# Mask by matmul up to pair 19, by copied gate sums from pair 20 on, and the later order planned again

## The chip, the cores and the metric

The kernel runs on one core of a Trainium2 chip. The metric is the device time of one execution in microseconds (us). The kernel before was timed in three runs: 425.29, 425.94 and 428.68, with the median 425.94. One further execution was taken by the profiler, and the traces below are from that one.

## The reference

Two layers follow each other. The first is attention with forgetting gates: 8 batches, 8 heads, 576 positions, head dimension 64. The second is a SwiGLU feed-forward block on 4608 tokens, 512 wide inside and 1536 wide in the middle.

```python
scores = scale * q @ k.T
cum = cumsum(log(clip(f, 1e-4, 1)))
decay = cum[:, :, :, None] - cum[:, :, None, :]
scores = where(causal, -1e9, scores + decay)     # causal: key after query
attn = exp(scores - max(scores)); attn = attn / (sum(attn) + 1e-9)
x = (attn @ v)  # heads side by side: 4608 x 512
out = (silu(x @ w_gate) * (x @ w_val)) @ w_out
```

The gate sum of the query's own position is the same for a whole row of scores, so the softmax drops it. Only the sum at the key has to be added.

## The kernel before, in words

Attention goes by 32 pairs of heads, two heads of one batch each. A pair has nine blocks of 64 queries; the two heads lie on the 128 partitions, so that one score matmul of a block `i` gives 128 rows by 64(i+1) keys. A pair is worked on in two groups: g = 0 holds the blocks 0 to 3, g = 1 the blocks 4 to 8. The scores are written with the opposite sign, so that a row's minimum is looked for and the exponential takes scale -1.

The steps of one pair are these.

- SyncE loads k, q and the pair's gate sums (`cb`, one row for each head, repeated on 64 partitions). GpSimd casts k and q to bf16 (`kb`, `qb`, L433 and L431), TensorE transposes them (L447), and ScalarE or VectorE copies the result out (`kt`, `qz`, L459 and L461).
- `scores` (L480): TensorE multiplies into one of two score banks (`sp`, L493). VectorE adds the gate sums, writes the sum into `t` and reads out the minimum of each row (L517, one custom instruction and one read of its accumulator). ScalarE takes the exponential and its row sum (L532).
- `normalize` (L538): VectorE makes the reciprocal of the sums (L548, L550), GpSimd scales the exponentials to bf16 (`pk`, L568), and the result is transposed: on TensorE for pairs 0 to 7 (L598), by one DMA transpose a pair for the others (L581).
- `weighted` (L606): TensorE multiplies with v (L624), and ScalarE or VectorE copies the result to the ring `xT` (L648).

The causal mask concerns only the last 64 keys of each block, the diagonal. There are two ways for it, and `MFROM` is the pair from which the second is used:

- Below `MFROM`, TensorE adds the mask to the scores: after each block's last score matmul comes one more, with the identity as weights and the mask of 64 columns as the moving side (L497). VectorE can then take the whole block in one instruction.
- From `MFROM` on, `copies` (L468) makes `cm`, the pair's gate sums plus the mask, once for all nine blocks, on VectorE or GpSimd (L476). VectorE then takes the diagonal 64 keys of a block by an instruction of its own that reads `cm` and goes on from the minimum of the part before it. Of the nine blocks, seven (1 to 7) are cut in two by this; block 0 is all diagonal, and block 8 has its diagonal in another bank in any case.

The feed-forward layer runs between: `gate` (L691) multiplies with the two weights (L706), ScalarE takes a tanh (L712), VectorE makes two products (L714, L717); `project` (L720) multiplies with the third (L734), and the result leaves through ScalarE or VectorE (L741, L743) and SyncE (L746).

The order of all this is fixed before the launch by `Plan.order` (L62). It takes a planned duration for each operation on each engine that may run it, a latency behind it, the buffers, and a priority; it plays the work through, always taking the operation that can start first, and writes the instructions of each engine in that order. Each engine keeps its order on the chip and waits where an operand isn't there. `NUDGE` (L259) shifts the priority of named units: a9.0 is pair 9, group 0; q is a pair's loading and transposing; f and o are tiles of the feed-forward layer. So a planned duration that is altered changes where everything behind it stands.

Of the kernel before, what the change touches and what calls it, by code (L numbers as in the profile page):

```python
# [8 lines left out]
F32 = mybir.dt.float32  # L9
BF16 = mybir.dt.bfloat16  # L10
AF = mybir.ActivationFunctionType
ALU = mybir.AluOpType
# [2 lines left out]
BIG = 1.0e9  # L15
HUGE = 3.0e38
COLD = 25000


class Op:  # L20
# [11 lines left out]
class Plan:  # L32
# [29 lines left out]
    def order(self):  # L62
# [72 lines left out]
        while ready:  # L135
            best = None
            for n, r in ready.items():
                o = self.ops[n]
                got = room(o, r)
                if got is None:  # L140
                    continue
                for e, dur in o.engs.items():
                    s = max(r, got[0], free[e])
                    for k in o.reads:
                        if k in using and using[k][0] != e:
                            s = max(s, using[k][1])
                    c = (s + o.bias.get(e, 0), o.prio, n, e, dur, got[1])
                    if best is None or c[:4] < best[:4]:
                        best = c
            if best is None:  # L150
                raise RuntimeError("no operation can start: " + ", ".join(str(self.ops[n].writes) for n in list(ready)[:20]))
            s, _, n, e, dur, take = best
            o = self.ops[n]
            s -= o.bias.get(e, 0)
            if e == "PE" and s < COLD:
                dur *= 2
            for k, b in take:
                name = self.home[k]
                self.where[k] = b
                slots[name][b] = k  # L160
                taken[name, self.line[k]] += 1
            o.start, o.eng = s, e
            free[e] = s + dur
            for k in o.reads:
                if self.home.get(k) in self.banks:
                    using[k] = e, s + dur + 30
            if o.dma:
                q = e == "POOL"
                at = max(wire[q], s + (2550 if q else 2000))
                both = max(0, min(2 * o.dma, wire[not q] - at))  # L170
                wire[q] = at + o.dma + both / 2
                wire[not q] += both / 2
                if o.ring:
                    free[e] = max(free[e], wire[q] - 1450)
                o.end = wire[q] + 1100
            else:
                o.end = free[e] + o.lat
            for k in {*o.writes, *o.reads, *o.holds}:
                left[k] -= 1
                until[k] = max(until[k], o.end)  # L180
            del ready[n]
            for kid in kids.get(n, ()):
                waiting[kid.n] -= 1
                if not waiting[kid.n]:
                    ready[kid.n] = max(d.end for d in kid.deps)
            done.append(o)
# [10 lines left out]
def kernel(  # L197
# [12 lines left out]
    B, H, S, D = q.shape  # L210
# [3 lines left out]
    P = 128  # L214
# [19 lines left out]
             [[(8, 0, 512)], [(8, 512, 576), (6, 0, 448)], [(7, 0, 512)], [(5, 0, 384)], [(4, 0, 320)]]]  # L234


    MFROM = 12
    CMENG = ("POOL", "DVE")

    ON_PE = {(p, g) for p in range(8) for g in range(2)}  # L240

    NDIRECT = 0
    NSEL = 1
    MOST = (("p", 1), ("o", 2), ("f", 3))
# [11 lines left out]
    HEAD = "10 00 20 30 11 01 31 21"  # L256


    NUDGE = "a21.0:1 a31.1:10 f5:1 f7:4.5 o8:2 q11:-2 q15:4 q24:2.5"  # L259

    WAIT = ""
    ORDER = [(int(u[0]), int(u[1])) for u in HEAD.split()]
# [32 lines left out]
    for i in range(0, NB, 2):  # L295
        bufs(f"e{i}", [P, QB * (i + 2)], F32, 2)
    bufs("eo", [P, 512], F32, 4)
    bufs("tm", [P, NB + 1], F32, 6)
    bufs("ls", [P, NB, 2], F32, 6)
    bufs("lr", [P, NB], F32, 6)  # L300
    both = {}
    for n in ("pk", "pT"):
        both[n] = [sb.tile([P, sum(NSL), P], BF16, name=f"{n}{x}") for x in range(2)]
# [114 lines left out]
    def prepare(p):  # L418
        s = first[p]
        for name in ("k", "q"):  # L420
# [4 lines left out]
            def cast(e, name=name, fk=fk, bk=bk, KR=KR):  # L425
# [5 lines left out]
                    eng[e].tensor_scalar(dst, src, -scale, 1.0, op0=ALU.mult, op1=ALU.mult)  # L431
                else:
                    eng[e].tensor_copy(dst, src)  # L433
            engs = {"POOL": 850}
            if p < NPB:
                engs = {"POOL": 850, "ACT": 850, "DVE": 500} if name == "k" else {"POOL": 1050, "ACT": 1050, "DVE": 680}
            o = pl.op(engs, cast, [fk], [bk], s - 1 + (name == "q") * .1)
# [30 lines left out]
    def copies(p):  # L468

        if p < MFROM:  # L470
            return
        pl.key(("cm", p), "cm")

        def add(e):
            src = pl.buf(("cb", p)).rearrange("r (i c) -> r i c", c=QB)
            eng[e].tensor_tensor(pl.buf(("cm", p)), src, maskf.unsqueeze(1).to_broadcast((P, NB, QB)), op=ALU.add)  # L476
        cost = {"POOL": S * 1.05 + 245, "DVE": S / .96 + 82}
        pl.op({e: cost[e] for e in CMENG}, add, [(("cb", p), 3)], [("cm", p)], first[p] - .5, holds=[("cb", p)])

    def scores(p, g):  # L480
        s = at[p, g]
        pl.key(("tm", p, g), "tm")
        pl.key(("ls", p, g), "ls")
        for n, bank in enumerate(BANKS[g]):
            sk = ("sp", p, g, n)
            pl.key(sk, "sp")
            pr = s + n * .05

            def mult(e, bank=bank, sk=sk):
                sp, kt, qz, o = pl.buf(sk), pl.buf(("kt", p)), pl.buf(("qz", p)), 0  # L490
                for i, a, z in bank:
                    last = z == QB * (i + 1)
                    nc.tensor.matmul(sp[:, o:o + z - a], qz[:, i, :, :].rearrange("p h r -> p (h r)"), kt[:, a:z],  # L493
                                     start=True, stop=not last or p >= MFROM)
                    o += z - a
                    if last and p < MFROM:
                        nc.tensor.matmul(sp[:, o - QB:o], ident, mask, start=False, stop=True)  # L497
            cols = [z - a for _, a, z in bank] + [64 for i, a, z in bank if z == QB * (i + 1) and p < MFROM]
            pl.op({"PE": mm(*cols)}, mult, [("kt", p), ("qz", p), (("kt", p), "done"), (("qz", p), "done"), "mask"], [sk], pr, lat=220)
            o = 0  # L500
            cuts = []
            for i, a, z in bank:
                last = z == QB * (i + 1)
                if last and a < QB * i and p >= MFROM:
                    cuts += [(i, a, QB * i), (i, QB * i, z)]
                else:
                    cuts.append((i, a, z))
            for i, a, z in cuts:
                last = z == QB * (i + 1)
                own = last and p >= MFROM  # L510
                tk = ("t", p, i)
                if a == 0:
                    pl.key(tk, "t")

                def add(e, i=i, a=a, z=z, o=o, sk=sk, tk=tk, last=last, own=own):
                    tm = pl.buf(("tm", p, g))
                    nc.vector.tensor_tensor_reduce(  # L517
                        out=pl.buf(tk)[:, a:z], in0=pl.buf(sk)[:, o:o + z - a],
                        in1=pl.buf(("cm", p))[:, i, :] if own else pl.buf(("cb", p))[:, a:z], scale=1.0,
                        scalar=HUGE if a == 0 else tm[:, NB:NB + 1], op0=ALU.add, op1=ALU.min,  # L520
                        accum_out=tm[:, i:i + 1] if last else tm[:, NB:NB + 1])
                w = [tk, ("tm", p, g)] + ([("m", p, i)] if last else [("m", p, i, "part")])
                r = [sk] + ([("cm", p)] if own else [(("cb", p), 3)]) + ([("m", p, i, "part")] if a else [])
                pl.op({"DVE": (z - a) / .96 + (142 if a else 82)}, add, r, w, pr, lat=100, holds=[] if own else [("cb", p)])
                o += z - a
                if last:
                    ek = ("e", p, i)
                    pl.key(ek, epool(i))

                    def exp(e, i=i, tk=tk, ek=ek):  # L530
                        L = QB * (i + 1)
                        nc.scalar.activation(pl.buf(ek)[:, :L], pl.buf(tk)[:, :L], AF.Exp,  # L532
                                             bias=pl.buf(("tm", p, g))[:, i:i + 1], scale=-1.0,
                                             accum_out=pl.buf(("ls", p, g))[:, i, 0:1])
                    sums[p, g] = pl.op({"ACT": QB * (i + 1) * .833 + 290}, exp, [tk, ("m", p, i)], [ek, ("ls", p, g)],
                          pr, lat=150, holds=[("tm", p, g)])

    def normalize(p, g):  # L538
# [10 lines left out]
        pl.op({"DVE": 95, "ACT": 200}, guard, [("ls", p, g)] + ([("z", "ls", n) for n in range(6)] if p < 3 else []), [("lr", p, g)], s, lat=120)  # L549
        pl.op({"DVE": 95}, lambda e: nc.vector.reciprocal(lr(), lr()), [("lr", p, g)], [("l2", p, g)], s, lat=170, holds=[("lr", p, g)])  # L550
        kk = ("pk", p, g)
        joint = not any((p, x) in ON_PE for x in range(2))
        pl.key(kk, f"pk{g}", same=("pk", p, 1 - g) if joint else None)
        w = HI[g] - LO[g] + 1
        for i in range(HI[g], LO[g] - 1, -1):
# [75 lines left out]
    def spread(p, g, pv):  # L631
# [5 lines left out]
        for a, z in ((0, cut), (cut, w)):  # L637
# [3 lines left out]
            def evac(e, a=a, z=z):  # L641
# [5 lines left out]
                src = bass.AP(src.tensor, src.offset + QB * (z - a - 1), [full[0], [-QB, z - a], full[2]])  # L647
                (nc.scalar.copy if e == "ACT" else nc.vector.tensor_copy)(dst, src)  # L648
            tok = t0 + a * QB, t0 + z * QB
            o = pl.op({"ACT": QB * (z - a) * .833 + 130, "DVE": QB * (z - a) / .96 + 85}, evac, [xk],  # L650
                      [("x", hp, n) for n in range(tok[0] // QB, tok[1] // QB)], s)
            o.bias = LATER if p >= 8 else {}
            evacs.append((pv, tok))
# [1 line left out]
    def load_v(b):  # L655
        for c in range(5):
# [9 lines left out]
                (), [fk], s, dma=1460 if n == P else 800, after=wait)  # L666
            def cast(e, c=c, n=n, fk=fk):
                (nc.scalar.copy if e == "ACT" else eng[e].tensor_copy)(pl.buf(("vt", b))[0:n, c, :, :], pl.buf(fk)[0:n, :, :])
            o = pl.op({"POOL": 670} if b else {"POOL": 670, "ACT": 580, "DVE": 600}, cast,
                  [fk] + ([("z", "vt", b)] if c == 4 and b < 2 else []), [("vt", b), ("vt", b, c)], s + .5)  # L670
            o.bias = SPARE

# [183 lines left out]
```

## Time and profile before

| | |
|---|---|
| median of three runs | 425.94 us |
| profiled execution, own time | 422.99 us |
| its span (first to last instruction) | 421.1 us |
| TensorE matmul busy | 397.9 us, 3124 matmuls |
| VectorE busy | 349.9 us, 1329 instructions |
| ScalarE busy | 318.6 us |
| GpSimd busy | 269.3 us |
| mask matmuls (L497) | 108 |
| copies with the mask (L476) | 12 on VectorE, 8 on GpSimd |

The profiled execution lies 2.95 us under the median, of which 1.89 us of its own time are outside the span. A busy TensorE in these rows includes the modelled end of each matmul, so one that is shown as busy can still have waited for a moment ahead of a matmul. Buffer numbers are left out in the names.

### The profile page before, as it was taken

What the parts mean: (1) busy time and instruction counts of PE and PEld (TensorE: products, weight loads), DVE (VectorE), ACT (ScalarE), POOL (GpSimd) and SP (SyncE); (2) the same over time, 40 slices, a digit from 0 to 9 for tenths busy, and PEclk for the clock granted to TensorE, in tenths of its full rate; (3) what the DMA queues carried; (4) which work ended last, traced back from release to release, by engine and by line L of the source; (5) the groups of instructions that cost most, each with busy time, mean ns of one, the idle gap of its engine ahead of it and who ended that gap; (6) DMA issues with size and microseconds to landing.
All of it is one profiled execution on the core that took longest, in us unless ns stands there. A gap on an engine that the chain in (4) does not pass through costs nothing.

```text
span 421.1 us, 10007 instructions
## 1 busy us (share of the span) xinstructions
PE 397.9 (94%) x3124; PEld 226.6 (54%) x3124; DVE 349.9 (83%) x1329; ACT 318.6 (76%) x882; POOL 269.3 (64%) x468
## 2 busy tenths in 40 slices
PE   2579999999999999999999999999999999999996
PEld 1446888665555555444544455454544444457675
DVE  4699999989998999899998999899989972765132
ACT  4599999999987989878998898798897843332221
POOL 7399978999985968767798696777964630000000
PEclk9999999999999999999999999999999999999999
DMA  7999999997999999999897999989948234000121
GB/s 199 197 151 248 213 213 208 230 233 181 203 205 198 262 189 225 225 247 190 175 228 187 235 208 214 221 193 188 224 113 166 57 85 115 2 25 27 51 76 50
DMA packets 143029, 72.21 MB, mean 171 GB/s; under 512 B 117760, under 2 KB 129792, under 8 KB 142976
## 3 DMA queue, kind: packets, MB, share of 16 engines
q1 hardware_dynamic: 136804, 66.27, 72.4%
q0 software_dynamic: 5808, 4.72, 7.5%
q10 hardware_dynamic: 364, 0.59, 0.5%
q8 instruction: 24, 0.39, 0.4%
q14 instruction: 29, 0.24, 0.2%
HBM read 47.04 MB, written 9.58 MB: 134 GB/s over the span
## 4 chain that ended last, share of the span: by engine, by line
PE 65%; DVE 18%; ACT 4%; issue 4%; DMA 4%; POOL 3%; SPq 0%; DVEq 0%; ACTq 0%; POOLq 0%
PE gv L706 33%; PE gv L734 16%; DVE t L517 10%; PE sp L493 7%; PE tx L624 4%; DMA qf<-in_q_dram 3%; DVE th L714 3%; PE tx L447 3%; DVE hh L717 3%; PE gv L598 2%; POOL pk L568 2%; ACT e L532 1%; ACT eo L532 1%; DVE qz L461 1%; DVE tm L517 1%
## 5 line engine op out<-in xcount | busy, mean ns | idle before, releaser
L568 POOL TENSOR_SCALAR pk<-e,lr 128x512 bf16<-128x512 f32 (+3 forms) x190 | 104.3, 552 | 55.6 <-issue 15.5
L517 DVE CUSTOM_DVE_ANT_0 t<-sp,cb 128x320 f32<-128x320 f32 (+7 forms) x268 | 121.0, 461 | 12.8 <-PE sp L493 1.7
L706 PE MATMUL gv<-xT,wv 128*128 128x512 bf16 (+2 forms) x576 | 111.2, 326 | 0.7 <-DVE th L714 0.6
L706 PE MATMUL gv<-xT,wg 128*128 128x512 bf16 (+2 forms) x576 | 111.4, 326 | 0.0
L734 PE MATMUL gv<-wo,hh 128*128 128x512 bf16 (+1 forms) x444 | 105.2, 373 | 0.0
L532 ACT ACTIVATE e<-t,tm 128x64 f32<-128x64 f32 (+4 forms) x160 | 88.6, 555 | 10.5 <-DVE tm L517 9.8
L714 DVE SCALAR_TENSOR_TENSOR th<-th,gv 128x512 f32<-128x512 f32 x108 | 73.8, 683 | 26.5 <-ACT th L712 25.8
L712 ACT ACTIVATE th<-gv 128x512 f32<-128x512 f32 x108 | 63.6, 590 | 32.5 <-PE gv L706 30.9
L532 ACT ACTIVATE eo<-t,tm 128x256 f32<-128x256 f32 (+3 forms) x128 | 71.3, 558 | 15.5 <-DVE tm L517 13.4
L493 PE MATMUL sp<-kt,qz 128*128 128x448 bf16 (+4 forms) x320 | 73.3, 293 | 6.6 <-DVE tm L517 5.8
L717 DVE TENSOR_TENSOR hh<-th,gv 128x512 bf16<-128x512 f32 x108 | 73.8, 684 | 4.2 <-PE gv L706 1.3
L568 POOL TENSOR_SCALAR pk<-eo,lr 128x256 bf16<-128x256 f32 (+3 forms) x128 | 68.2, 533 | 6.7 <-DVE tm L517 3.3
L706 PEld LDWEIGHTS <-wv 128*128 128x128 bf16 x576 | 50.6, 98 | 38.1 <-issue 3.6
L706 PEld LDWEIGHTS <-wg 128*128 128x128 bf16 x576 | 50.4, 98 | 36.8 <-issue 0.6
L734 PEld LDWEIGHTS <-hh 128*128 128x128 bf16 x444 | 41.0, 98 | 40.2 <-issue 1.0
L493 PEld LDWEIGHTS <-qz 128*128 128x128 bf16 x320 | 30.6, 100 | 27.3 <-issue 5.2
L517 DVE CUSTOM_DVE_ANT_0 t<-sp,cm,tm 128x64 f32<-128x64 f32 x160 | 42.2, 278 | 2.1 <-PE sp L493 0.2
L741 ACT ACTIVATE ot<-gv 128x512 f32<-128x512 f32 (+1 forms) x33 | 19.0, 578 | 25.5 <-PE gv L734 25.0
L517 DVE DVE_READ_ACCUMULATOR2_ANT tm<- 128x1 f32 x460 | 38.1, 83 | 0.0
L431 POOL TENSOR_SCALAR qb<-qf 72x1024 bf16<-72x1024 f32 x30 | 31.2, 1040 | 6.2 <-DMA qf<-in_q_dram 5.3
L459 ACT COPY qz<-tx 64x576 bf16<-64x576 bf16 x46 | 28.9, 628 | 3.5 <-PE tx L447 3.0
L532 ACT ACTIVATION_READ_ACCUMULATOR e<-t,tm 128x1 f32 x160 | 30.5, 191 | 0.0
(64 smaller groups left out, 403.1 us busy)
## 6 DMA issues: line engine op xcount, KB each, us to landing
out_dram<-ot SPq DMA_DIRECT2D x35, 256.0 KB
kf<-in_k_dram SPq DMA_DIRECT2D x31, 288.0 KB
qf<-in_q_dram SPq DMA_DIRECT2D x31, 288.0 KB
cb<-cum_f SPq DMA_DIRECT2D x62, 144.0 KB
vf<-in_v_dram SPq DMA_DIRECT2D x32, 256.0 KB
wo<-in_moe_w_out_dram POOLq DMA_DIRECT2D x3, 512.0 KB, 10.8
vf<-in_v_dram SPq DMA_DIRECT2D x8, 128.0 KB
wv<-in_moe_w_val_dram POOLq DMA_DIRECT2D x2, 512.0 KB, 7.6
```

The source lines that it names most:

```text
L431: eng[e].tensor_scalar(dst, src, -scale, 1.0, op0=ALU.mult, op1=ALU.mult)
L459: nc.scalar.copy(dst, src)
L493: nc.tensor.matmul(sp[:, o:o + z - a], qz[:, i, :, :].rearrange("p h r -> p (h r)"), kt[:, a:z], start=True, stop=not last or p >= MFROM)
L517: nc.vector.tensor_tensor_reduce(out=pl.buf(tk)[:, a:z], in0=pl.buf(sk)[:, o:o + z - a], in1=pl.buf(("cm", p))[:, i, :] if own else pl.buf ...
L532: nc.scalar.activation(pl.buf(ek)[:, :L], pl.buf(tk)[:, :L], AF.Exp, bias=pl.buf(("tm", p, g))[:, i:i + 1], scale=-1.0, accum_out=pl.buf(( ...
L568: eng[e].tensor_scalar(dst, src, r, 1.0, op0=ALU.mult, op1=ALU.mult)
L706: nc.tensor.matmul(pl.buf(bk)[:, j * n:j * n + n], wt[:, ko, fc * P:fc * P + P], xT[:, ko, x0:x0 + n], start=ko == 0, stop=ko == KD - 1)
L712: pl.op({"ACT": 487}, lambda e, u=u: nc.scalar.activation(pl.buf(("th", t, u)), pl.buf(("wg", t, u)), AF.Tanh, scale=0.5), [("wg", t, u)], ...
L714: pl.op({"DVE": 605}, lambda e, u=u: nc.vector.scalar_tensor_tensor(pl.buf(("th", t, u)), pl.buf(("th", t, u)), 1.0, pl.buf(("wg", t, u)), ...
L717: pl.op({"DVE": 605}, lambda e, u=u: nc.vector.tensor_mul(pl.buf(("hh", t, u)), pl.buf(("th", t, u)), pl.buf(("wv", t, u))), [("u", t, u), ...
L734: nc.tensor.matmul(pl.buf(bk)[:, 0:z - a], hh[:, (fc % nf) * n + ms * P:(fc % nf) * n + ms * P + P], wo[:, fc, a:z], start=fc == 0, stop=f ...
L741: nc.scalar.mul(pl.buf(ok)[:, a:z], pl.buf(bk)[:, 0:z - a], 0.5)
```

## The change

`MFROM` goes from 12 to 20, so the pairs 12 to 19 are masked by TensorE too. The planner gets other durations: a copy with the mask 1350 ns on GpSimd and 710 on VectorE (from 850 and 682); a cast of k or q 800 and 1010 on GpSimd from pair 8 on (from 850 both); a cast of v 590 from the third batch on (from 670); the copy to `xT` on ScalarE 80 ns less from pair 8 on; VectorE's work 3% longer behind the first 100 us of the plan; the latency behind L517 140 in place of 100 from pair 8 on. `NUDGE` has 22 entries where it had 8. The buffers `lr` go from 6 to 5. The minimum of a cut block's first part has a column for each block in `tm`, where it had one for all. `TWO` is off, so what stands under it makes no instruction. `JFROM = 8` says the same as the expression that it replaces.

```diff
+SLOW = 1.03
...
+            if e == "DVE" and s > 100000:
+                dur *= SLOW
...
-    MFROM = 12
+    MFROM = 20
...
+    JFROM = 8
+    TWO = False
...
-    NUDGE = "a21.0:1 a31.1:10 f5:1 f7:4.5 o8:2 q11:-2 q15:4 q24:2.5"
+    NUDGE = "a9.0:2 a10.0:0.5 a13.0:0.5 a14.1:-1 a20.0:1 a21.0:1 a29.0:-1 a30.1:4 a31.1:10 f3:7 f5:1 f7:4.5 o2:-1.5 o4:1 o6:1.5 o8:2 q11:-0.5 q15:4 q19:-1 q24:2.5 q25:0.5 q28:-3"
...
-    bufs("tm", [P, NB + 1], F32, 6)
+    bufs("tm", [P, 2, NB], F32, 6)
...
-    bufs("lr", [P, NB], F32, 6)
+    bufs("lr", [P, NB], F32, 5)
...
-            engs = {"POOL": 850}
+            engs = {"POOL": 850 if p < 8 else 800 if name == "k" else 1010}
...
-        cost = {"POOL": S * 1.05 + 245, "DVE": S / .96 + 82}
+        cost = {"POOL": 1350, "DVE": 710}
...
-                        scalar=HUGE if a == 0 else tm[:, NB:NB + 1], op0=ALU.add, op1=ALU.min,
-                        accum_out=tm[:, i:i + 1] if last else tm[:, NB:NB + 1])
+                        scalar=HUGE if a == 0 or two else tm[:, 1, i:i + 1], op0=ALU.add, op1=ALU.min,
+                        accum_out=tm[:, int(not last), i:i + 1])
...
-                pl.op({"DVE": (z - a) / .96 + (142 if a else 82)}, add, r, w, pr, lat=100, holds=[] if own else [("cb", p)])
+                pl.op({"DVE": (z - a) / .96 + (142 if a and not two else 82)}, add, r, w, pr, lat=100 if p < 8 else 140, holds=[] if own else [("cb", p)])
...
-            o = pl.op({"ACT": QB * (z - a) * .833 + 130, "DVE": QB * (z - a) / .96 + 85}, evac, [xk],
+            o = pl.op({"ACT": QB * (z - a) * .833 + (130 if p < 8 else 50), "DVE": QB * (z - a) / .96 + 85}, evac, [xk],
...
-            o = pl.op({"POOL": 670} if b else {"POOL": 670, "ACT": 580, "DVE": 600}, cast,
+            o = pl.op({"POOL": 670 if b < 2 else 590} if b else {"POOL": 670, "ACT": 580, "DVE": 600}, cast,
```

More of the change, by code (lines that the diff above doesn't have):

```diff
@@ L513, in scores, with add @@
                     pl.key(tk, "t")
-                def add(e, i=i, a=a, z=z, o=o, sk=sk, tk=tk, last=last, own=own):
+                two = TWO and p >= MFROM and (not last or a > 0)
+                def add(e, i=i, a=a, z=z, o=o, sk=sk, tk=tk, last=last, own=own, two=two):
                     tm = pl.buf(("tm", p, g))
@@ L519, in add, with least @@
                         in1=pl.buf(("cm", p))[:, i, :] if own else pl.buf(("cb", p))[:, a:z], scale=1.0,
-                        scalar=HUGE if a == 0 else tm[:, NB:NB + 1], op0=ALU.add, op1=ALU.min,
-                        accum_out=tm[:, i:i + 1] if last else tm[:, NB:NB + 1])
-                w = [tk, ("tm", p, g)] + ([("m", p, i)] if last else [("m", p, i, "part")])
-                r = [sk] + ([("cm", p)] if own else [(("cb", p), 3)]) + ([("m", p, i, "part")] if a else [])
-                pl.op({"DVE": (z - a) / .96 + (142 if a else 82)}, add, r, w, pr, lat=100, holds=[] if own else [("cb", p)])
+                        scalar=HUGE if a == 0 or two else tm[:, 1, i:i + 1], op0=ALU.add, op1=ALU.min,
+                        accum_out=tm[:, int(not last), i:i + 1])
+                w = [tk, ("tm", p, g)] + ([("m", p, i, a)] if two else [("m", p, i)] if last else [("m", p, i, "part")])
+                r = [sk, ("cm", p) if own else (("cb", p), 3)] + ([("m", p, i, "part")] if a and not two else [])
+                pl.op({"DVE": (z - a) / .96 + (142 if a and not two else 82)}, add, r, w, pr, lat=100 if p < 8 else 140, holds=[] if own else [("cb", p)])
+                if last and two:
+                    def least(e, i=i):
+                        m = pl.buf(("tm", p, g))[:, :, i:i + 1]
+                        eng[e].tensor_scalar(m[:, 0, :], m[:, 1, :], m[:, 0, :], None, op0=ALU.min)
+                    pl.op({"POOL": 150}, least, [("m", p, i, 0), ("m", p, i, a)], [("m", p, i)], pr - .5, lat=120, holds=[("tm", p, g)])
                 o += z - a
@@ L532, in exp @@
                         nc.scalar.activation(pl.buf(ek)[:, :L], pl.buf(tk)[:, :L], AF.Exp,
-                                             bias=pl.buf(("tm", p, g))[:, i:i + 1], scale=-1.0,
+                                             bias=pl.buf(("tm", p, g))[:, 0, i:i + 1], scale=-1.0,
                                              accum_out=pl.buf(("ls", p, g))[:, i, 0:1])
@@ L551, in normalize @@
         kk = ("pk", p, g)
-        joint = not any((p, x) in ON_PE for x in range(2))
+        joint = p >= JFROM
         pl.key(kk, f"pk{g}", same=("pk", p, 1 - g) if joint else None)
```

## The prediction

> **What bounds the kernel now.** The first view is the page's span and busy shares.
>
> ```profile
> span 421.1 us, 10007 instructions
> PE 397.9 (94%) x3124; PEld 226.6 (54%) x3124; DVE 349.9 (83%) x1329; ACT 318.6 (76%) x882; POOL 269.3 (64%) x468
> ```
>
> TensorE is busy in 94% of the span. The share is an average, though, so the second view is busy time by stage. The columns are TensorE, its weight loads, VectorE, ScalarE, GpSimd, each with its count, then clock, DMA share, GB/s. I cut at 121.5 and 210 us because just 80 score matmuls lie between (last row), ten for each of the pairs 12 to 19, which are the pairs that change their masking.
>
> ```profile
> 0.00:30.00 30.00, 15.34 (x126) 10.99 (x127) 19.38 (x72) 19.52 (x56) 19.67 (x56) 1.00 0.93 184
> 30.00:121.50 91.50, 90.24 (x944) 62.15 (x942) 88.36 (x308) 88.63 (x247) 83.88 (x140) 1.00 1.06 216
> 121.50:210.00 88.50, 87.41 (x624) 43.85 (x623) 82.80 (x357) 75.70 (x217) 66.06 (x108) 1.00 1.02 212
> 210.00:343.00 133.00, 130.03 (x878) 64.18 (x877) 123.82 (x544) 112.18 (x326) 98.33 (x164) 1.00 0.85 181
> 343.00:421.10 78.10, 74.87 (x559) 45.47 (x556) 35.49 (x52) 22.52 (x39) 1.32 (x3) 1.00 0.17 52
> ...
> 121.50:210.00 88.50, 17.19 (x80) 7.36 (x81) 1.00 1.02 212
> ```
>
> More than half of what TensorE lacks lies in the first 30 us. In the pairs 12 to 19 it shows 1.1 us idle of 88.5, VectorE 5.7. The granted clock is full everywhere. The third view is what TensorE waited for in this stretch (us in total, times, longest).
>
> ```profile
> PE tx L447 <- POOL qb L431: 0.4, 1, 0.4
> PE gv L706 <- DVE th L714: 0.2, 1, 0.2
> PE sp L493 <- DVE tm L517: 0.2, 1, 0.2
> ```
>
> About half of the 0.8 us named is waiting for VectorE. But a matmul's modelled end hides short waits, so I also work out what TensorE would need without any. The chain of waits in pair 9, one of the pairs that already mask by matmul, gives the pace, and the windows by line give the counts: L706, L734, L447 and L624, first from 121.5 to 210 and then from 210 to 343.
>
> ```profile
> 98.02 0.86 PE gv L706 x4
> 98.88 0.14 PE sp L493
> 99.02 0.03 PE sp L497
> 99.05 0.11 PE sp L493
> ...
> 121.50:210.00 88.50, 46.52 (x194) 18.02 (x192) 1.00 1.02 212
> 121.50:210.00 88.50, 22.82 (x92) 8.42 (x92) 1.00 1.02 212
> 121.50:210.00 88.50, 7.02 (x118) 6.06 (x118) 1.00 1.02 212
> 121.50:210.00 88.50, 8.77 (x140) 5.95 (x140) 1.00 1.02 212
> ...
> 210.00:343.00 133.00, 71.45 (x294) 27.61 (x294) 1.00 0.85 181
> 210.00:343.00 133.00, 36.78 (x148) 13.59 (x148) 1.00 0.85 181
> 210.00:343.00 133.00, 8.02 (x134) 6.97 (x134) 1.00 0.85 181
> 210.00:343.00 133.00, 11.41 (x182) 7.72 (x182) 1.00 0.85 181
> ```
>
> Four matmuls of 512 columns take 0.86 us, 0.215 each or 0.42 ns a column. In the stretch of pairs 12 to 19 stand 194 + 92 = 286 such matmuls: 61.5 us. A pair's ten score matmuls have 64 x 45 = 2880 columns by the blocks' sizes, 1.21 us, so 9.7 for eight pairs. The 118 small transposes have 72 or 96 columns, about 35 ns: 4.1. The products with v are taken at their busy 8.8. That is 84.1 of 88.5, so **4.4 us at most are lost to waits** in this stretch. From 210 to 343 the same sum is 442 x 0.215 + 12 x 1.21 + 134 x 0.035 + 11.4 = 125.6 of 133, so 7.4 at most. TensorE bounds the kernel, and behind the start about 12 us of it are waits.
>
> **The change part by part.**
>
> *Masks by matmul, added.* Eight pairs with nine blocks give 72 more matmuls of L497. Each takes 0.03 us on the chain above (99.02 to 99.05; 64 columns at 0.42 ns and a little), and the score matmul ahead of it takes no longer for it (0.14 us for 320 columns is 0.42 ns a column). So 72 x 0.029 = **2.1 us of TensorE work**, and TensorE has no cover for it: it counts in full. The bounds are 0 (all of it in waits that are there anyway) and 7.4, if each weight load of the identity stood open, by the row of these loads:
>
> ```profile
> L497 PEld LDWEIGHTS <-ident 128*128 128x128 bf16 x108 | 10.6, 103 | 6.1 <-issue 3.7
> ```
>
> I take 2.1, because the pace of the chain is a direct measurement of the same operation in the same place. The Trainium skill speaks against it: TensorE: Matmul & The Clock Gate, section LDWEIGHTS, puts a load of 128 columns at about 107 ns, and its section on the mechanism of packing says that a load runs beside a matmul only when the two use different row groups. By that rule the 72 masks would cost an estimated 7.7 us. The load's mean of 103 ns agrees with the figure, but the 0.03 us from one matmul to the next doesn't agree with the rule: here the loads ran beside matmuls of the same rows.
>
> *Cut blocks, removed.* In eight pairs seven blocks each are no longer cut: 56 VectorE instructions and 56 reads of the accumulator go. The price of one is read from VectorE's timeline. The first two rows are an uncut 512 in pair 11 and what follows, the others a cut 448 + 64 in pair 12.
>
> ```profile
> 115.05 0.69 DVE L517 CUSTOM_DVE_ANT_0 t<-sp,cb 128x512 f32<-128x512 f32 x1
> ...
> 115.66 0.69 DVE L714 SCALAR_TENSOR_TENSOR th<-th,gv 128x512 f32<-128x512 f32 x1
> ...
> 126.08 0.62 DVE L517 CUSTOM_DVE_ANT_0 t<-sp,cb 128x448 f32<-128x448 f32 x1
> ...
> 126.75 0.28 DVE L517 CUSTOM_DVE_ANT_0 t<-sp,cm,tm 128x64 f32<-128x64 f32 x1
> 126.96 0.08 DVE L517 DVE_READ_ACCUMULATOR2_ANT tm<- 128x1 f32 x1
> ```
>
> Uncut 0.61 us (115.05 to 115.66), cut 0.88 (126.08 to 126.96). So 0.27 is saved where the two parts follow each other. Where something stands between, the second part alone (126.75 to 126.96, 0.21) goes, against 64 more keys in the whole (0.61 / 8 = 0.08): 0.13. For 56 that is 7 to 15 us of VectorE.
>
> *Copies with the mask, fewer.* Counted in the changed kernel's order, 4 of 12 go from VectorE and 4 of 8 from GpSimd:
>
> ```profile
> L476 POOL TENSOR_TENSOR cm<-cb,maskf 128x576 f32<-128x576 f32 x8 | 11.3, 1409 | 0.0
> L476 DVE TENSOR_TENSOR cm<-cb,maskf 128x576 f32<-128x576 f32 x12 | 10.3, 859 | 0.2
> ...
> L461 DVE COPY qz<-tx 64x576 bf16<-64x576 bf16 x18 | 13.6, 754 | 1.3 <-PE tx L447 0.7 <-ACT qz L459 0.3
> ```
>
> That is 3.4 us of VectorE and 5.6 of GpSimd. Against it, five copies of `kt` and `qz` go from ScalarE to VectorE by the new order, 3.8 us by the last row. VectorE is relieved by 7 + 3.4 - 3.8 = 7 to 15 us, nearly all in this stretch. What it is worth is only the wait of TensorE that it ends: between 0 and 4.4 us. Of the waits named there, half were for VectorE, so I take **2.2**. Behind the relief the queue for GpSimd (0.4 of the 0.8) is late next.
>
> *New durations and nudges.* Up to pair 9's first group the order of TensorE is as before. From there to pair 12 four to eight wide matmuls come earlier. Then, between the first scores of pair 12 and of pair 20, the changed order has 244 wide feed-forward matmuls where there were 284: 40 x 0.215 = 8.6 us of filler moves behind pair 20. It isn't saved, it is done later, and at pair 31 both orders have nearly the same amount behind them. The pairs 12 to 19 follow each other in about 88.5 - 8.6 + 2.1 - 2.2 = 80 us, 10.0 a pair where it was 11.1. For the later 133 us the new placing can win or lose; the bounds are -7.4 (all waits gone) and the same upwards, and I take 0, since the operations and their waits there are of the same kind. The last 400 matmuls stand as they were, so the end costs nothing either way.
>
> *Buffers.* `lr` with 5 holds two and a half pairs. The scaling that reads it must be done within two pairs anyway, as the exponentials have no more buffers, so I take 0 and no loss. `tm` with a column for each block: 0, its writer and reader are the same engine in the same order.
>
> **Sum.** +2.1 - 2.2 + 0 = -0.1 us on a span of 421.1 in an execution of 422.99. The runs have their median 2.95 above that execution, so I put the difference on the median: 425.94 - 0.1, rounded **426 us**.
>
> **The rivals.**
>
> *The new order also ends later waits, so it is faster.* The planner had a GpSimd copy at 850 ns where the row of L476 above shows 1409, and the new price of 1350 is nearer. If all 4.4 us of the stretch and half of the 7.4 behind it go, the time is 425.94 + 2.1 - 4.4 - 3.7 = 419.9. For it: VectorE's busy 93% in both stretches, which makes TensorE wait in many small pieces. Against it: these waits need not be the planner's doing, and 6.4 us of 11.8 must go for over 1%.
>
> *The transfers can't follow the closer pairs, so it is slower.* Filler that is taken out of the stretch brings the same loads and DMA transposes into less time. The DMA share there is 1.02 over 88.5 us; in 80 us it is 1.13. The highest over 20 us before is this:
>
> ```profile
> 240.00:260.00 20.00, 1.00 1.14 223
> ```
>
> Whether 1.13 holds for 80 us, no row shows. If the engines give no more than 1.08, half way, the stretch takes 88.5 x 1.02 / 1.08 = 83.6 us, TensorE stands idle for 3.6 with its filler placed elsewhere, and 425.94 + 2.1 + 3.6 = 431.6. At no more than 1.02 it is 8.5 idle and 436.5. It decides from about 1.10 down. Against it: a burst of 1.14 was carried with TensorE fully busy.
>
> *The weight loads stand open.* 72 x 0.103 more on the 2.1: 435.4. It is the rule of the skill cited above; the chain speaks against it.
>
> That the change doesn't do what it says is excluded by the order: 72 masks more, 56 cut blocks fewer.
>
> **How the numbers follow.** Forecast 0.65: relief between 0 and 4.4 and up to 2 either way behind it, 422 to 430. Faster rival 0.15, transfers 0.18, weight loads 0.02. The range that should hold 8 in 10 goes from 420.5, near the faster rival's time, to 431.5, near the transfers' at 1.08. One per cent, 4.3 us, is about what a measurement of this kernel tells from no change, since its three runs lie 3.4 apart: 421.7 to 430.2 is "same". The forecast lies nearly all within, with a third of the faster rival and a sixth of the transfers: 0.72. Faster 0.10, slower 0.18.
>
> **What would show it.** TensorE busy higher by about 2 us, 180 matmuls of L497, still 0.03 us apart from the next. VectorE's busy lower by some 7 to 15. The 80 score matmuls of pairs 12 to 19 in about 80 us. Less wait of L493 for L517 there. If transfers rule, GpSimd's casts wait for `qf` and `kf`, TensorE's L447 waits for the casts, and DMA share there stays under 1.10. The prediction is wrong if TensorE's idle time behind the first 30 us changes by more than 4 us.

## The result, and the profile after

The changed kernel is faster: the ratio to the kernel before is 0.9885, 95% interval 0.9858 to 0.9912, over 18 runs each. The ratio leaves out executions that fell into a slower state; the medians over all 18, 421.56 and 425.89 us, lie 4.3 us apart. Taken once more on another occasion the ratio was 0.9857 (0.9808 to 0.9906). On 425.94 us the first ratio is 4.9 us. The forecast was no change; the time itself lies in the range, near its lower end.

The first profile of the changed kernel (span 422.6) has a stall of TensorE before 50 us, which the last section shows. The rows here are from its second profile (span 416.8), which like that of before has none there. First the page's span and busy shares, then the windows by stage. The stage borders are moved so that the second row again ends where pair 12 begins, and the third holds the 80 score matmuls of the pairs 12 to 19. Lines are those of the changed kernel: L498 scores, L502 masks, L526 VectorE's sum and minimum, L452 transposes of q and k, L638 products with v.

```profile
span 416.8 us, 9933 instructions
PE 394.6 (95%) x3196; PEld 228.5 (55%) x3196; DVE 338.2 (81%) x1214; ACT 315.5 (76%) x881; POOL 262.5 (63%) x464
...
0.00:30.00 30.00, 15.08 (x122) 10.82 (x123) 18.77 (x70) 18.92 (x54) 19.35 (x54) 1.00 0.91 179
30.00:124.90 94.90, 92.56 (x965) 63.33 (x964) 90.46 (x312) 90.20 (x252) 82.03 (x139) 1.00 1.00 210
124.90:201.40 76.50, 76.50 (x622) 40.47 (x621) 66.85 (x239) 66.80 (x202) 60.06 (x107) 1.00 1.03 220
201.40:340.00 138.60, 136.91 (x931) 68.89 (x929) 128.14 (x546) 117.25 (x338) 99.67 (x165) 1.00 0.89 188
340.00:416.80 76.80, 73.60 (x563) 45.02 (x560) 33.94 (x51) 22.36 (x39) 1.39 (x3) 1.00 0.17 53
...
124.90:201.40 76.50, 17.12 (x80) 7.38 (x81) 1.00 1.03 220
```

The pairs 12 to 19 take 76.5 us where they took 88.5, and TensorE is busy in every one of them. VectorE is busy for 66.9 of the 76.5, 87% where it was 94%. Over the whole span VectorE lost 11.7 us and GpSimd 6.8. What TensorE waited for behind pair 20 is this:

```profile
PE sp L498 <- DVE tm L526: 1.5, 1, 1.5
PE tx L452 <- POOL qb L436: 0.2, 1, 0.2
```

In the stretch ahead of it the same view shows no wait of TensorE at all. Where many short waits stood, one of 1.5 us is left.

The busy rows hide short waits, so I take them from the trace, matmul by matmul: the time from one start to the next, less the columns at the pace of an undisturbed stream. Before, TensorE so lost 1.9 us from 30 to 121.5, 3.8 in pairs 12 to 19, and 6.3 behind. In the changed kernel it lost 3.2, 0.0 and 2.1. That is 12.0 against 5.3, 6.7 us less; 72 masks at 0.029 us put 2.1 on; 4.6 us remain, and the spans differ by 4.3. **The gain is waits of TensorE that ended, less the masks.** The experiments ask which part of the change ended them.

### The profile page after: what moved, and what is told of

Same layout as the page of the kernel before. It is cut to its first block, busy times and chain, and to the rows that moved or that the text cites. A ratio compares the mean times of both kernels' runs of the same rounds, so it can differ in the third digit from the quotient of the medians.

```text
span 422.6 us, 9933 instructions
## 1 busy us (share of the span) xinstructions
PE 396.7 (94%) x3196; PEld 229.1 (54%) x3196; DVE 337.1 (80%) x1214; ACT 316.1 (75%) x881; POOL 262.8 (62%) x464
## 4 chain that ended last, share of the span: by engine, by line
PE 78%; DMA 8%; ACT 5%; POOL 4%; DVE 3%; issue 1%; SPq 0%; POOLq 0%; DVEq 0%
PE gv L720 38%; PE gv L748 20%; PE sp L498 7%; PE tx L638 6%; PE tx L452 3%; DMA pT<-pk 2%; DMA vf<-in_v_dram 2%; PE gv L612 2%; POOL pk L582 2%; ACT eo L546 2%; DMA qf<-in_q_dram 2%; ACT e L546 2%; DMA kf<-in_k_dram 1%; DVE t L526 1%; ACT th L726 1%
## 5 line engine op out<-in xcount | busy, mean ns | idle before, releaser
L526 DVE CUSTOM_DVE_ANT_0 t<-sp,cb 128x320 f32<-128x320 f32 (+7 forms) x276 | 123.6, 466 | 16.4 <-PE sp L498 5.8
L582 POOL TENSOR_SCALAR pk<-e,lr 128x128 bf16<-128x128 f32 (+3 forms) x190 | 101.6, 538 | 46.8 <-DVE tm L526 19.8
L546 ACT ACTIVATE e<-t,tm 128x576 f32<-128x576 f32 (+4 forms) x160 | 88.9, 557 | 10.5 <-DVE tm L526 8.7
L582 POOL TENSOR_SCALAR pk<-eo,lr 128x256 bf16<-128x256 f32 (+3 forms) x128 | 69.9, 546 | 9.9 <-DMA pT<-pk 4.2
L498 PE MATMUL sp<-kt,qz 128*128 128x448 bf16 (+5 forms) x320 | 71.5, 294 | 3.6 <-DVE tm L526 3.5
L498 PEld LDWEIGHTS <-qz 128*128 128x128 bf16 x320 | 30.6, 100 | 21.9 <-issue 0.9
L526 DVE DVE_READ_ACCUMULATOR2_ANT tm<- 128x1 f32 x404 | 33.4, 83 | 0.0
L638 PE MATMUL tx<-pT,vt 128*64 128x320 bf16 (+4 forms) x448 | 29.6, 266 | 3.8 <-POOL vt L682 1.5
L638 PEld LDWEIGHTS <-vt 128*64 128x64 bf16 x448 | 19.1, 110 | 21.0 <-issue 11.8
```

Source lines behind the costliest of these rows:

```text
L526: nc.vector.tensor_tensor_reduce(out=pl.buf(tk)[:, a:z], in0=pl.buf(sk)[:, o:o + z - a], in1=pl.buf(("cm", p))[:, i, :] if own else pl.buf ...
L582: eng[e].tensor_scalar(dst, src, r, 1.0, op0=ALU.mult, op1=ALU.mult)
L638: nc.tensor.matmul(xo[r, 0:QB * n], vt[:, c, 2 * hp + h, :], pT[:, a:a + n, 64 * h:64 * h + 64], start=(c == 0), stop=(c == nch - 1))
```

## The experiments

The ratios are to the kernel before, with 95% intervals; a difference of 0.001 is 0.43 us.

**The changed kernel again.** No edit; its rows are above. Measured 0.9857 (0.9808 to 0.9906).

> The changed kernel once more, for a second profile beside the next ones on one chip. Ratio to before 0.986 to 0.991. If its later stretch (pairs 20 to 31) keeps TensorE's waits of the score matmuls for VectorE under 1 us where before has several, the order theory for that stretch stands; if they are as before, the first profile owed it to its stall near 45 us.

The later stretch has 1.5 us of waits for VectorE in one piece, a little over the "under 1" that was asked, but the many short ones are gone in this profile too. So they aren't owed to the stall in the first profile.

**Masks and uncut blocks at the old order.** The plan is that of the kernel before, instruction by instruction; only what pairs 12 to 19 issue is altered. Their copies with the mask go too.

```diff
+    EMIT = 20
-                                     start=True, stop=not last or p >= MFROM)
+                                     start=True, stop=not last or p >= EMIT)
-                    if last and p < MFROM:
+                    if last and p < EMIT:
                         nc.tensor.matmul(sp[:, o - QB:o], ident, mask, start=False, stop=True)
...
+                    if MFROM <= p < EMIT and 0 < i < 8:
+                        if a:
+                            return
+                        z, last = QB * (i + 1), True
+                    own = own and p >= EMIT
...
+            if p < EMIT:
+                return          # in copies: no copy for these pairs
```

> Kernel before in its own planned order; in pairs 12 to 19 alone the mask comes by the 72 matmuls, each block is taken by VectorE in one instruction at the place of its first part, and the copies with the mask go. Relief theory (the uncut blocks made the gain): ratio about 0.990 of before. Order theory (the new plan made it): about 1.000, 2.1 us of masks against about 2 us of waits ended. The trace should show 180 of L497 and less VectorE by 10 us or more in both.

Measured 0.9966 (0.9931 to 1.0001). Between the two: the masking itself is worth about 1.4 us without any new order, so relief of 3.5 (2.1 to 5.0 by the interval) against 2.1 of masks. VectorE's first instructions of pair 12 and of pair 20 lie 87.1 us apart, 88.4 before, though 2.1 us of masks were added. The waits that are left show what this kernel doesn't gain: behind pair 20 TensorE still waits for VectorE in seven places, as it did before. First the row of this kernel (L496 is its score matmul, L525 VectorE), then that of the kernel before.

```profile
PE sp L496 <- DVE tm L525: 2.5, 7, 0.7
```

```profile
PE sp L493 <- DVE tm L517: 1.8, 7, 0.4
```

**Cut blocks at the new order.** The plan of the changed kernel, but VectorE takes the blocks of pairs 12 to 19 in two parts.

```diff
+                    if 12 <= p < 20 and 0 < i < 8:
+                        m = QB * i
+                        for x, y in ((0, m), (m, z)):
+                            nc.vector.tensor_tensor_reduce(
+                                out=pl.buf(tk)[:, x:y], in0=pl.buf(sk)[:, o + x:o + y], in1=pl.buf(("cb", p))[:, x:y], scale=1.0,
+                                scalar=tm[:, 1, i:i + 1] if x else HUGE, op0=ALU.add, op1=ALU.min,
+                                accum_out=tm[:, int(not x), i:i + 1])
+                        return
```

> Changed kernel in its own order; in pairs 12 to 19 VectorE takes the blocks 1 to 7 in two parts again (56 more instructions, 7 to 15 us of VectorE), masked by matmul as in the changed kernel. Relief theory: the gain is lost, ratio to before 1.000 or above. Order theory: the gain mostly stays, ratio 0.989 to 0.993.

Measured 1.0000 (0.9964 to 1.0036): the whole gain is gone, so the new order alone doesn't make it. But this kernel has the cut blocks and pays the 2.1 us for 72 masks as well, which the kernel before does not. By the relief theory it would so take 1.005; that it takes 1.000 means that the new order earns about 2.1 us (0.6 to 3.6) without the uncut blocks; part of it may come from the copies with the mask, which stay away here. Its stage row for pairs 12 to 19 shows VectorE at 94% again, and 82.1 us in place of 76.5:

```profile
124.70:206.80 82.10, 78.25 (x611) 40.93 (x620) 77.37 (x351) 68.71 (x204) 59.75 (x106) 1.00 0.98 211
```

VectorE has 10.5 us more to do in the stretch, and 5.6 of it come through to its length. Behind pair 20 the waits stay ended: this kernel's view names the same single wait as the changed kernel's, where before there were seven.

```profile
PE sp L498 <- DVE tm L534: 1.5, 1, 1.5
```

From VectorE's first instruction of pair 20 to the end it takes 215.6 us, the changed kernel, in the same order, 214.8. The same sum from start to start, for the score matmuls alone that start over 8 ns late and whose last release came from VectorE, puts the four kernels side by side (us, one profile of each):

| | pairs 12 to 19 | behind them |
|---|---|---|
| before: cut blocks, old order | 2.5 | 5.4 |
| masks, uncut blocks, old order | 0.0 | 5.4 |
| masks, cut blocks, new order | 5.0 | 2.5 |
| changed: masks, uncut blocks, new order | 0.0 | 1.7 |

**The uncut blocks end the waits in pairs 12 to 19, at either order. The new order ends most of those behind, with cut blocks too.** In pairs 12 to 19 cut blocks cost more at the new order, which has less filler between the scores, 5.0 against 2.5. By the times alone the relief at the new order, 4.9 us (3.0 to 6.8), can't be told from the 3.5 at the old one.

**Masks twice.** The same mask added again on the diagonal; the exponential of a masked score is 0 either way.

```diff
+                        if p >= 12:
+                            nc.tensor.matmul(sp[:, o - QB:o], ident, mask, start=False, stop=False)
                         nc.tensor.matmul(sp[:, o - QB:o], ident, mask, start=False, stop=True)
```

> Changed kernel in its own order with each mask matmul of pairs 12 to 19 issued twice (72 more of 64 columns). If a mask costs its 0.029 us in full, 2.1 us more than the changed kernel: ratio to before 0.993 or 0.994. If masks hide in waits: 0.988 as the changed kernel. If weight loads stood open, 7 us more: 1.005.

Measured 0.9898 (0.9858 to 0.9938), beside 0.9857 and 0.9885 of the changed kernel. As time alone it can't tell 2.1 us from 0.6, only that open weight loads are out. The stage row can: the same 239 instructions of VectorE now take 78.5 us where they took 76.5.

```profile
124.90:203.40 78.50, 77.61 (x682) 42.50 (x693) 66.91 (x239) 67.28 (x202) 60.05 (x106) 1.00 1.09 215
```

2.0 us for 72 masks is 0.028 each. TensorE pays each in full, as it stands without a wait there.

**Only MFROM, and only the planner.** Four kernels are planned anew with single parts of the change. The first two keep `MFROM = 12`, the third has all of the change but `MFROM`, the fourth has nothing but `MFROM`.

```diff
 # VectorE's margins alone
+            if e == "DVE" and s > 100000:
+                dur *= SLOW
-                ..., add, r, w, pr, lat=100, ...
+                ..., add, r, w, pr, lat=100 if p < 8 else 140, ...
 # GpSimd's durations alone
-            engs = {"POOL": 850}
+            engs = {"POOL": 850 if p < 8 else 800 if name == "k" else 1010}
-        cost = {"POOL": S * 1.05 + 245, "DVE": S / .96 + 82}
+        cost = {"POOL": 1350, "DVE": 710}
-            o = pl.op({"POOL": 670} if b else ...
+            o = pl.op({"POOL": 670 if b < 2 else 590} if b else ...
 # all but MFROM: the changed kernel with
-    MFROM = 20
+    MFROM = 12
 # MFROM alone: the kernel before with
-    MFROM = 12
+    MFROM = 20
```

> Kernel before with two planner numbers of the change alone: VectorE 3% longer behind 100 us and latency 140 behind L517 from pair 8 on. MFROM stays 12, nudges as before. Order theory, with the pessimism for VectorE as its cause: waits of L493 for L517 behind 120 us fall from several us to under 1, ratio about 0.993. If the cause is another part of the plan or the relief: 1.000, waits as before.

> Kernel before with the GpSimd durations of the change alone, MFROM = 12 and old nudges. If the durations are worth something without the relief, ratio 0.992 or less; if the gain needs both, 0.998 to 1.01.

> Changed kernel with MFROM = 12 again, planned anew with all other durations, margins and nudges of the change. If the new order alone is worth some 4 us, ratio 0.990; if it needs the relief of VectorE, 1.000 or slower, with the score matmuls waiting for VectorE by 2 us or more in pairs 12 to 19.

> Kernel before with MFROM = 20 as its only edit, planned again by its old durations and nudges. The plan moves 64 wide matmuls behind pair 20 by itself. Relief with moved filler as the whole cause: 0.990. If the tuned durations and nudges are needed: 0.997 or above, as the masks at the old order gave.

Measured: margins alone 1.0350 (1.0304 to 1.0396), durations alone 1.0052 (1.0006 to 1.0097), all but `MFROM` 1.0016 (0.9967 to 1.0065), `MFROM` alone 1.0078 (1.0032 to 1.0124). None is faster, but the traces say more than the times. In all but `MFROM` no score matmul waits for VectorE behind pair 20; the four waits that its view names lie all in pairs 12 to 19, where the blocks are still cut:

```profile
PE sp L498 <- DVE tm L526: 3.0, 4, 0.9
```

There TensorE stalls from 184 us on, and from 188 to 198 its granted clock is 0.51. All ten executions of this kernel have a mean granted clock from 0.980 to 0.992, those of the kernel before, taken beside them, from 0.992 to 1.000. So this plan too ends the later waits of the scores, but loses time in pairs 12 to 19; what begins the stall there wasn't tested.

Margins alone was a miss of the theory that they end the waits of the scores. That kernel's attention ends late (the last score at 357.5 us, 336.7 before), and near the end TensorE waits for the last pairs' transposes:

```profile
PE sp L496 <- DVE tm L520: 7.1, 8, 1.3
PE tx L627 <- DMA pT<-pk: 6.3, 2, 5.2
```

Its clock was granted at half three times for 6.8 us, at 191, 283 and 368 us, which is up to 10 of the 15 us that it is slower.

**What MFROM needs beside it.** With `MFROM = 20`: first the new durations (GpSimd's and the copy to `xT`) with the old nudges and no margins; then the margins alone; then all of the change with the old nudges; then all of it without margins.

```diff
 # durations only: the kernel before with MFROM = 20, GpSimd's durations as above, and
-            o = pl.op({"ACT": QB * (z - a) * .833 + 130, ...
+            o = pl.op({"ACT": QB * (z - a) * .833 + (130 if p < 8 else 50), ...
 # margins only: the kernel before with MFROM = 20 and VectorE's margins as above
 # old nudges: the changed kernel with
+    NUDGE = "a21.0:1 a31.1:10 f5:1 f7:4.5 o8:2 q11:-2 q15:4 q24:2.5"
 # no margins: the changed kernel with
-SLOW = 1.03
+SLOW = 1.0
-                ..., lat=100 if p < 8 else 140, ...
+                ..., lat=100, ...
```

> Kernel before with MFROM = 20 and the measured durations of the change (casts, copies with the mask, copy to xT), without the margins for VectorE, with the nudges of before. If true GpSimd durations are what MFROM = 20 alone lacked (it took 1.008), ratio about 0.986 and no wait of L447 for GpSimd's casts in pairs 12 to 19. If the margins are, about 1.005.

> Kernel before with MFROM = 20 and the two margins for VectorE of the change (3% behind 100 us, latency 140), with the old durations of GpSimd and the old nudges. If the margins are what MFROM = 20 alone lacked, ratio about 0.986; if the durations of GpSimd are, about 1.005 with L447 waiting for its casts.

> Changed kernel with the nudges of before, all else of the change kept. If the nudges carry the order's share, ratio 0.998 or above; if relief and moved filler carry it, 0.990 to 0.993, since this order too has some 40 wide matmuls fewer ahead of pair 20.

> Changed kernel, planner without the two margins for VectorE (no 3%, latency 100 in place of 140), nudges of the change kept. If the margins make the order's share of the gain (some 4 us), ratio about 0.998 and the score matmuls wait more in pairs 20 to 31. If the relief in pairs 12 to 19 with the filler moved behind pair 20 makes it, about 0.990.

| `MFROM = 20`, old nudges | old durations | new durations |
|---|---|---|
| no margins | 1.0078 (1.0032 to 1.0124) | 1.0124 (1.0026 to 1.0221) |
| margins | 1.0014 (0.9966 to 1.0062) | 0.9853 (0.9772 to 0.9934) |

With the new nudges and new durations but no margins: 0.9855 (0.9816 to 0.9894). The cell of durations without margins rests on three executions. The lower right cell, like the changed kernel and the one without margins, also has `lr` at 5 and the other `tm`; the planner gives the same order with 5 and with 6 `lr`, but no run has these two alone. Both theories about a single part fall, since neither margins nor durations alone make `MFROM = 20` faster. Durations with margins do, and so do durations with the new nudges. TensorE's waits behind 121.5 us show what each part ends. They are of `MFROM` alone, then of margins only, then of both with the old nudges (scores are L493, L496 and L498; transposes of q and k L447 and L450).

```profile
PE sp L493 <- DVE tm L517: 1.9, 4, 0.9
PE tx L624 <- DMA pT<-pk: 1.9, 1, 1.9
PE tx L447 <- POOL kb L433: 1.8, 2, 1.5
PE sp L493 <- DVE qz L461: 0.6, 1, 0.6
PE tx L447 <- DVE xT L648: 0.6, 1, 0.6
PE tx L447 <- POOL qb L431: 0.4, 1, 0.4
```

```profile
PE tx L450 <- POOL qb L434: 1.8, 2, 0.9
PE tx L450 <- POOL kb L436: 1.2, 3, 0.5
PE sp L496 <- DVE tm L520: 0.9, 2, 0.7
```

```profile
PE tx L638 <- DMA pT<-pk: 0.5, 1, 0.5
PE sp L498 <- DVE tm L526: 0.5, 1, 0.5
PE gv L720 <- DVE th L728: 0.2, 1, 0.2
```

With the old durations the transposes wait for GpSimd's casts, 2.2 us in the first and 3.0 in the second. With the margins the scores' waits for VectorE fall from 1.9 to 0.9 in these rows. With both, no wait for the casts is named, and 0.5 for VectorE. The sum from start to start, of score matmuls late for VectorE behind pair 20, sorts the runs the same way (us, one profile of each):

| the planner has | late for VectorE behind pair 20 |
|---|---|
| neither | 5.4 (before), 5.4 (masks at the old order), 5.8 (`MFROM` alone) |
| new durations | 6.4 (`MFROM = 12`), 8.1 (`MFROM = 20`, a profile at a clock of 0.95, the pace scaled to it), 3.8 (no margins, new nudges) |
| margins | 5.0 (`MFROM = 12`), 2.5 (`MFROM = 20`) |
| both | 0.0 (all but `MFROM`), 0.7 (old nudges), 1.7 (changed kernel) |

So margins and durations together end most of these waits, at either `MFROM`. It isn't the whole account: the kernel without margins is as fast with 3.8 of them left in its profile, and every planned number shifts the whole order.

What the runs do settle: the masks cost 2.1 us. The uncut blocks are worth 3.5 us (2.1 to 5.0) at the old order. The new order is worth about 2.1 us (0.6 to 3.6) without them and 3.4 (1.6 to 5.3) with them, through the waits behind pair 20. That a plan and the relief gain more together than the sum of both isn't shown. None of the three plans at `MFROM = 12` came out faster in time. Which of GpSimd's durations matters most wasn't tried.

## Why the prediction was wrong

- **Masks: right.** +2.1 us was forecast by the pace in pair 9; doubling them lengthened the stretch by 2.0. The rival of open weight loads is out.
- **VectorE's relief in work: right in sum.** 7 to 15 us were forecast, the busy row fell by 11.7. The copies with the mask gave only 1.2 of the 3.4 that they were put at: the eight left on VectorE took 1134 ns each, where the twelve had taken 859.
- **What the relief is worth: mis-sized.** The step said "Of the waits named there, half were for VectorE, so I take 2.2", of 4.4 at most. Matmul by matmul 3.8 were lost there, and all 3.8 are gone. At the old order the relief alone measured 3.5, with its interval wide. The named waits were 0.8 us, the visible fifth of the lost time, and their split said nothing of the rest: of the 3.8, 2.7 were lost ahead of score matmuls, nearly all with VectorE as the last release.
- **The later stretch: the failed step.** The prediction took 0 "since the operations and their waits there are of the same kind". They are, and yet 4.2 of 6.3 us went. The order decides these waits: at the old order they stayed with the relief (5.4 us of scores late for VectorE, as before), at the new one most went without it (2.5). Which planned number does it is shown only as far as the table above goes. The sum with both terms right is 2.1 - 3.8 - 4.2, and 1.3 more lost ahead of pair 12: -4.6, against -4.3 in the spans.
- **The length of the stretch: too long.** 80 us were forecast, it is 76.5, near the TensorE work of the changed order (76.0) with no wait. Of the 3.5, 1.6 is the relief, and 1.6 are transposes and products with v that the new order puts elsewhere (98 for 118, and 7.9 us for 8.8).
- **The faster rival** was this, with 419.9 us and the right two terms; it was given 0.15. The argument against it, that the waits need not be the planner's doing, rested on no row.
- **The transfers: out.** The DMA share in the stretch was 1.03, not 1.13. The forecast spread the old stretch's transfers over fewer microseconds; instead the next stretch has 0.89 where it had 0.85, which fits loads that run ahead and transposes that follow behind. And 1.14 was not the highest over 20 us before: from 30 to 50 us it was 1.18.

## What to carry to other kernels

Where the first engine shows 99% busy and still loses time, sum the time from start to start against the pace of an undisturbed stream and sort the loss by what follows it; the waits that a view names may be a fifth of it. A change that also alters the order is two changes. To tell them apart, issue the new instructions at the old order and the old ones at the new order, and count what each still pays: here both pay 2.1 us of masks. Then compare stage by stage and not only the total, for the second came out at 1.000 and had still kept most of the gain behind pair 20. Plan again with the durations checked against the trace; with `MFROM = 20` and the old nudges the plan came out at 1.008 with the old durations and no margins, and at 0.985 with the new durations and margins.

## What the runs showed of the hardware

Short idle times of TensorE cost its clock here too. In the first profile of the changed kernel a load of v, issued at 32.67 us, holds GpSimd's cast until 42.19 (the chain of waits, first rows), and the casts and scalings behind it hold TensorE. The windows after it have the columns of the stage table, with the granted clock behind GpSimd's share:

```profile
32.67 9.46 DMA vf<-in_v_dram
42.13 0.05 issue
42.19 0.61 POOL vt L682
42.80 2.81 POOL pk L582 x5
...
40.00:42.00 2.00, 1.40 (x15) 0.79 (x12) 1.92 (x6) 2.00 (x6) 0.00 (x0) 1.00 1.11 237
42.00:44.00 2.00, 0.93 (x10) 0.56 (x10) 1.41 (x7) 1.21 (x4) 1.81 (x4) 1.00 1.15 272
44.00:46.00 2.00, 0.90 (x8) 0.53 (x8) 0.36 (x2) 1.51 (x5) 2.00 (x4) 1.00 1.13 246
46.00:48.00 2.00, 2.00 (x15) 1.53 (x13) 1.16 (x4) 0.10 (x1) 1.96 (x3) 0.54 0.92 142
48.00:50.00 2.00, 2.00 (x17) 1.66 (x16) 1.25 (x2) 1.63 (x5) 2.00 (x5) 0.61 1.20 201
50.00:52.00 2.00, 2.00 (x34) 1.65 (x34) 1.36 (x5) 1.47 (x4) 2.00 (x4) 1.00 1.02 274
```

TensorE was idle for 2.8 of 6 us by these rows, never for 2 us on end, and from 46 to 50 it was granted 0.54 and 0.61 of its clock, though busy throughout: 1.7 us more. The two windows hold one stretch at 0.50, from 46.2 to 49.6 us; in the 3.4 us ahead of it TensorE is shown busy for 2.0. The Trainium skill, TensorE: Matmul & The Clock Gate, section "What's actually happening", lets the clock fall to a half behind an idle window of about 3.4 us. Half the clock agrees with the 0.50; but here no idle time was that long, and a stretch that was partly busy was enough.
